# Blockwise attention and expert routing: ranks computed ahead of the scores, table compares on VectorE, zeros and the first v cast on ScalarE

## The chip, the cores and the metric

The kernel runs on one core of one Trainium2 chip. A core has five engines with queues of their own: TensorE (PE in the profile; its weight loads are PEld), VectorE (DVE), ScalarE (ACT), GpSimd (POOL) and SyncE (SP). SP, ACT and POOL also issue DMA transfers, all of which run on the same 16 DMA engines. The metric is device time in microseconds (us); several executions are timed and their median is taken. One execution is recorded by the hardware profiler, and every duration below is from that one.

## The reference

Attention has batch 8, 8 heads, 576 tokens and head dimension 64. A query sees a key if its block of 64 tokens is not before the key's block. The result becomes 4608 rows of 512, and each row goes through the two matrices of the expert that its domain number names:

```python
scores = np.where(block_i >= block_j, scale * q @ k.T, -1e9)
attn = softmax(scores)                       # float32
x = (attn @ v).transpose(0, 2, 1, 3).reshape(B * S, H * D)   # 4608 x 512
for e in range(8):                           # w1[e]: 512 x 1024, w2[e]: 1024 x 512
    mask = domain_id == e
    out[mask] = np.maximum(x[mask] @ w1[e], 0.0) @ w2[e]
```

All inputs and outputs are float32 (domain numbers are 64-bit integers); the kernel computes in float16 with float32 sums.

## The kernel before

The order of the work on each engine is the order in which the program writes it; no planner moves anything.

**Attention** is a loop over 32 pairs of heads (`p`, four pairs to a batch `b`) and a 33rd round that only finishes. A round of pair p contains, in this order: `emit_G(0)`, the first scores of p by TensorE and their exp by ScalarE; `emit_T(p + 2)`, the transposition of q and k of the pair after next by TensorE (L292) with two copies by VectorE (L296, tile QK); `emit_G(1)`; `emit_P`, the products with v of the pair before (L355, L360); `emit_G(2)`; `emit_Q`, the rest of them, then the reciprocal (L376) and the scaling (L377) into x by VectorE. After the last pair of a batch x is stored to the DRAM tensor x_rows by SP. In the last pair of a batch `emit_VE` (L386) copies part of the next batch's v into the tile VE by VectorE.

**Loads.** q and k are loaded by POOL with a cast to float16 (`load_qk`, four transfers a batch), v in float32 (`load_v`, five a batch) into vst, and cast to vS by `cast_v` (three instructions): for batch 0 by VectorE, for others by POOL. `loads(p)`, at the end of a round, writes batch b's loads at p = 4b - 10 and the cast of batch b - 1 between them. At p = 20 and 22 it issues the weights of experts 0 and 1, eight transfers each.

**Routing** (`routing`, a generator of which each round takes one step from p = 5) computes for each token its rank within its expert: a one-hot tile me, two matmuls (with ones_sq and the triangle up) that count over partitions, a scan on VectorE (L255), three POOL instructions (L259, L260, L264), a sum (L267), and `slot_col` (L211 to L224), integer arithmetic that makes the column u_f and the place lo_h of each token.

**The table** (`table`, `inverse`, one step a round from p = 19) inverts this: for each quarter of the tokens POOL builds one-hot tiles Hq (L165, L168), Hh (L170, L174) and L (L178, L182) by subtracting and comparing with zero, TensorE multiplies them (L188) and VectorE adds up (L193, L195). The result tok0 says which token stands in each of 128 x 40 slots, five blocks of 128 for each expert. L168, L170 and L182 are POOL's compares and its product.

**Experts.** POOL gathers the tokens of an expert from x_rows (L479, an indirect DMA for each block), TensorE transposes them (L489), VectorE copies (L492), `mm1` multiplies by w1 (L511) with relu by ScalarE (L517), `mm2` by w2 (L528); VectorE copies each block to a buffer osb (L534), POOL scatters it to the output (L535). Within mm2 POOL also issues the weights of expert e + 3 and TensorE transposes the next expert's tokens. For an expert with more than 640 tokens a loop from L590 makes further rounds; here it makes none.

Of the kernel before, what the change touches and what calls it, by code (L numbers as in the profile page):

```python
# [9 lines left out]
F32 = mybir.dt.float32  # L10
F16 = mybir.dt.float16
I32 = mybir.dt.int32
AF = mybir.ActivationFunctionType
ALU = mybir.AluOpType
# [4 lines left out]
def kernel(  # L19
# [54 lines left out]
    def load_v(eng, b, cs):  # L74
        for c in cs:
# [4 lines left out]

    load_qk(0, 0, 1)
    load_v(nc.sync, 0, range(5))
    nc.sync.dma_start(
        out=dom_i[:],
        in_=moe_domain_id.bitcast(I32).rearrange("(p c) -> p c", p=128))

    identh = const.tile([128, 128], F16, name="identh")
    make_identity(nc, identh[:])
    load_qk(0, 1, HP)
    up = const.tile([128, 128], F16, name="up")  # L90
    make_upper_triangular(nc, up[:], 1.0, diag=False)
    iota_h = const.tile([128, 128], F16, name="iota_h")
    nc.gpsimd.iota(out=iota_h[:], pattern=[[1, 128]], base=0, channel_multiplier=0,
                   allow_small_or_imprecise_dtypes=True)
    p_f = const.tile([128, 1], F32, name="p_f")
    nc.gpsimd.iota(out=p_f[:], pattern=[[0, 1]], base=4, channel_multiplier=NJ,
# [40 lines left out]
    cnt = const.tile([128, E], F32, name="cnt")  # L137
    tok0 = const.tile([128, 2, E * NB], I32, name="tok0")
    for i in range(3):
        nc.vector.memset(vS[i][:, :, :, 1:131:129], 1.0)  # L140
    for i in range(2):
        nc.vector.memset(ATE[i][:, 0:64], 1.0)
        nc.vector.memset(ATE[i][:, 64:832], 0.0)
        nc.vector.memset(VE[i][:], 0.0)
        nc.vector.memset(VE[i][0:64, :, :, 1:2], 1.0)
        nc.vector.memset(VE[i][64:128, :, :, 130:131], 1.0)
    po = aps.tile([128, 2, 512], F32, name="po")
    nc.vector.memset(po[:, 1, 264:396], 1.0)

    def inverse(sb, pp, tag, ncols, base, tok):
# [3 lines left out]
        inv = sb.tile([128, 2, ncols], F32, name="inv", tag="inv")  # L157
        yield
        for qt in range(4):
            js = slice(NQ * qt, NQ * qt + NQ)  # L160
            L = sb.tile([128, NQ, 128], F16, name="L", tag="L", bufs=2)
            Hq = sb.tile([128, NQ, ncols], F16, name="Hq", tag="Hq", bufs=2)
            Hh = sb.tile([128, NQ, 2, ncols], F16, name="Hh", tag="Hh", bufs=2)
            sh = [128, NQ, ncols]
            nc.gpsimd.tensor_tensor(  # L165
                out=Hq[:], in0=iota_h[:, 0:ncols].unsqueeze(1).to_broadcast(sh),
                in1=ub[:, js].unsqueeze(2).to_broadcast(sh), op=ALU.subtract)
            nc.gpsimd.tensor_scalar(  # L168
                out=Hq[:], in0=Hq[:], scalar1=0.0, scalar2=None, op0=ALU.is_equal)
            nc.gpsimd.tensor_scalar(  # L170
                out=Hh[:, :, 0], in0=Hq[:], scalar1=p_f[:, 0:1], scalar2=None,
                op0=ALU.mult)
            yield
            nc.gpsimd.tensor_tensor(  # L174
                out=Hh[:, :, 1], in0=Hq[:],
                in1=iota_h[:, js].unsqueeze(2).to_broadcast(sh), op=ALU.mult)
            sl = [128, NQ, 128]
            nc.gpsimd.tensor_tensor(  # L178
                out=L[:], in0=iota_h[:].unsqueeze(1).to_broadcast(sl),
                in1=lo_h[:, js].unsqueeze(2).to_broadcast(sl), op=ALU.subtract)  # L180
            yield
            nc.gpsimd.tensor_scalar(  # L182
                out=L[:], in0=L[:], scalar1=0.0, scalar2=None, op0=ALU.is_equal)
            yield
            ps = pp.tile([128, 512], F32, name=tag, tag=tag, bufs=2)
            pv = ps[:, 0 : 2 * ncols]
            for j in range(NQ):
                nc.tensor.matmul(  # L188
                    out=pv, lhsT=L[:, j], rhs=Hh[:, j].rearrange("p a c -> p (a c)"),
                    start=(j == 0), stop=(j == NQ - 1))  # L190
            fi = inv[:].rearrange("p a c -> p (a c)")
            if qt == 0:
                nc.vector.tensor_copy(out=fi, in_=pv)  # L193
            else:
                nc.vector.tensor_tensor(out=fi, in0=fi, in1=pv, op=ALU.add)  # L195
        nc.vector.tensor_tensor(
            out=inv[:, 0], in0=inv[:, 0], in1=inv[:, 1], op=ALU.add)
# [30 lines left out]
    def routing():  # L228
        nc.vector.memset(ones_sq[:], 1.0)
        dom_f = asb.tile([128, NJ], F16, name="dom_f")  # L230
# [3 lines left out]
            out=me[:], in0=iota_h[:, 0:E].unsqueeze(2).to_broadcast([128, E, NJ]),  # L234
            in1=dom_f[:].unsqueeze(1).to_broadcast([128, E, NJ]), op=ALU.is_equal)
        msk = asb.tile([128, E, NJ], F16, name="msk")
        nc.vector.memset(msk[:], 1.0)
        nc.vector.memset(msk[:, :, 0:1], 0.0)
        yield
        yield  # L240
        fl = "p e j -> p (e j)"
        nj = E * NJ
        ps_t = aps.tile([128, 512], F32, name="PT", tag="PT", bufs=2)
        ps_r = aps.tile([128, 512], F32, name="PT", tag="PT", bufs=2)
        nc.tensor.matmul(out=ps_t[:, 0:nj], lhsT=ones_sq[:],
                         rhs=me[:].rearrange(fl), start=True, stop=True)
        nc.tensor.matmul(out=ps_r[:, 0:nj], lhsT=up[:],
                         rhs=me[:].rearrange(fl), start=True, stop=True)
        rt = asb.tile([128, E, NJ], F32, name="rt")
        nc.scalar.copy(out=rt[:].rearrange(fl), in_=ps_t[:, 0:nj])  # L250
        rr = asb.tile([128, E, NJ], F32, name="rr")
        nc.scalar.copy(out=rr[:].rearrange(fl), in_=ps_r[:, 0:nj])
        yield
        inc = asb.tile([128, E, NJ], F32, name="inc")
        nc.vector.tensor_tensor_scan(  # L255
            out=inc[:].rearrange(fl), data0=msk[:].rearrange(fl),
            data1=rt[:].rearrange(fl), initial=0.0, op0=ALU.mult, op1=ALU.add)
        rk = asb.tile([128, E, NJ], F32, name="rk")
        nc.gpsimd.tensor_tensor(out=rk[:], in0=inc[:], in1=rt[:], op=ALU.subtract)  # L259
        nc.gpsimd.tensor_tensor(out=rk[:], in0=rk[:], in1=rr[:], op=ALU.add)  # L260
        yield
        nc.vector.tensor_scalar(out=cnt[:], in0=inc[:, :, NJ - 1], scalar1=-1.0,
                                scalar2=None, op0=ALU.add)
        nc.gpsimd.tensor_tensor(out=rk[:], in0=rk[:], in1=me[:], op=ALU.mult)  # L264
        yield
        rank = asb.tile([128, NJ], F32, name="rank")
        nc.vector.tensor_reduce(out=rank[:], in_=rk[:].rearrange("p e j -> p j e"),  # L267
                                axis=AX.X, op=ALU.add)
        yield
        ri = slot_col(asb, rank[:], dom_f[:], NJ, u_f[:], "t")  # L270
# [3 lines left out]
        nc.vector.tensor_copy(out=lo_h[:], in_=lo_i[:])  # L274
        yield
        nc.vector.memset(base_f[:], 0.0)
# [120 lines left out]

    npair = B * HP
    QKs = {0: emit_T(0)}
    rout, tabl = routing(), table()  # L400

    w1s, w2s = {}, {}


    def loads(p):
        fn = nc.gpsimd.tensor_copy
        for b in range(2, B):
            if p == max(0, 4 * b - 10):
                load_qk(b)
                load_v(nc.gpsimd, b, range(0, 3))  # L410
                cast_v(fn, b - 1)
                load_v(nc.gpsimd, b, range(3, 5))
        if p == 4 * B - 12:
            w1s[0], t1 = load_w1(wsb, 2, moe_w1[0])
            w2s[0], t2 = load_w2(wsb, 2, moe_w2[0])
            for f in t1:
                f()
            cast_v(fn, B - 1)
            for f in t2:
                f()  # L420
        if p == 4 * B - 10:
            w1s[1], t1 = load_w1(wsb, 2, moe_w1[1])
            w2s[1], t2 = load_w2(wsb, 2, moe_w2[1])
            for f in t1 + t2:
                f()

    prev = None
    for p in range(npair + 1):
        b, hp = divmod(p, HP)
        st = None  # L430
        if p < npair:
# [4 lines left out]
            emit_G(0, st)  # L436
        if p == 0:
            QKs[1] = emit_T(1)
            cast_v(nc.vector.tensor_copy, 0)
            emit_VE(0)  # L440
        elif p + 2 < npair:
            QKs[p + 2] = emit_T(p + 2)
# [6 lines left out]
        if prev is not None:  # L449
# [5 lines left out]
            elif prev["p"] % HP == HP - 1:  # L455
                store_x(prev, 0, DM, nc.sync)
        if p == 0:
            QKs[2] = emit_T(2)
        if p < npair and hp == 3 and b + 1 < B:
            emit_VE(b + 1)  # L460
        if p > 4:
            next(rout, None)
        if p > 18:
            next(tabl, None)
        loads(p)
        prev = st
    for _ in tabl:
        pass
    att.close()

# [51 lines left out]
    def mm2(hT, w2h, tok, dst, todo=(), nxt=None):  # L522
        if nxt is not None:
            transpose_block(*nxt, 0)
        for blk in range(NB):
# [5 lines left out]
            if nxt is not None and blk + 1 < NB:  # L531
                transpose_block(*nxt, blk + 1)
            osb = msb.tile([128, DM], F32, name="osb", tag="osb", bufs=6)
            nc.vector.tensor_copy(out=osb[:], in_=po[:])  # L534
# [102 lines left out]
```

## Time and profile before

| what | value |
|---|---|
| median of 14 runs | 346.28 us (341.71 to 348.49) |
| profiled execution, its own time | 343.2 us |
| its span | 341.4 us |
| granted TensorE clock, mean | 0.912 |
| busy: PE, DVE, ACT, POOL | 268.3, 157.0, 141.0, 227.2 us |
| last scaling of x (L377) ends | 158.2 us |
| first gather (L479) starts | 161.4 us |
| first matmul of expert 0 (L511) starts | 168.2 us |
| last scatter (L535) starts | 327.3 us |

A row of a timeline has the start, the duration (of a run of equal instructions from its first start to its last end), engine, line and operation, the tiles out<-in with partitions x elements, the count, and in brackets the idle time of the engine before it with what ended it. A row of a group has, after the count, its busy time and the mean nanoseconds of one, and after the second bar the idle time before. A row of the waits has the total, how often, and the longest. The granted clock is a share of full speed.

### The profile page before, as it was taken

Reading aid. Unit: us, or ns where it says so; the run is one execution under the profiler, and the core shown is the slowest. Engines: PE = TensorE matmul, PEld = TensorE weight load, DVE = VectorE, ACT = ScalarE, POOL = GpSimd, SP = SyncE. Lnnn points to the kernel's source line nnn. Section 1 sums busy time; section 2 is a strip of 40 time slices with the busy share of each in tenths; the row PEclk is TensorE's granted clock in tenths of the full one; section 3 lists DMA queues with packets and bytes.
Section 4 is the critical chain, followed back from the end, with each engine's and each line's share of the span. In section 5 each row is a group of like instructions: output and inputs, shape, how many; then the busy total and the mean of one; then the engine's idle time right before and its main releaser. Section 6 shows DMA issues by size and latency. Waiting matters only on the chain. (4 is left out here: it accounts for less than half of the span.)

```text
span 341.4 us, 8495 instructions
## 1 busy us (share of the span) xinstructions
PE 268.3 (79%) x3622; PEld 176.2 (52%) x3622; DVE 157.0 (46%) x277; ACT 141.0 (41%) x203; POOL 227.2 (67%) x273
## 2 busy tenths in 40 slices
PE   1589688768699297582589998989799899999920
PEld 1357456546466275462355665647465464756500
DVE  5467788878568956943102523040230504042210
ACT  1358758828678266470042331505123060514200
POOL 8758557986629999970787858787777775232220
PEclk9999989969989679785599999999999999999975
DMA  9999999999965996022369996989899695112120
GB/s 174 199 212 222 211 224 202 198 220 252 210 198 106 206 184 144 2 72 69 94 127 220 223 231 144 238 193 222 228 186 223 143 225 182 58 61 76 63 80 0
DMA packets 36023, 55.66 MB, mean 163 GB/s; under 512 B 9390, under 2 KB 22190, under 8 KB 35984
## 3 DMA queue, kind: packets, MB, share of 16 engines
q0 software_dynamic: 25680, 49.17, 68.9%
q1 hardware_dynamic: 9776, 5.81, 6.4%
q8 instruction: 29, 0.48, 0.6%
q10 hardware_dynamic: 528, 0.13, 0.2%
q14 instruction: 10, 0.08, 0.1%
HBM read 67.15 MB, written 15.20 MB: 241 GB/s over the span
## 5 line engine op out<-in xcount | busy, mean ns | idle before, releaser
L309 ACT ACTIVATE A<-ps 128x1024 f16<-128x1024 f32 (+1 forms) x96 | 82.9, 884 | 58.8 <-PE ps L304 46.5
L517 ACT ACTIVATE hT<-ph 128x640 f16<-128x640 f32 (+1 forms) x72 | 46.3, 644 | 117.8 <-PE ph L511 95.4
L528 PE MATMUL po<-w2h,hT 128*128 128x512 f16 x320 | 74.9, 379 | 6.0 <-DVE osb L534 4.9
L511 PE MATMUL ph<-xT,w1h 128*128 128x320 f16 x512 | 73.7, 304 | 1.8 <-issue 1.1
L535 POOL DMA_INDIRECT out_dram<-osb,tok x40 | 40.7, 1018 | 46.3 <-DVE osb L534 31.4
L492 DVE COPY xT<-pt 128x512 f16<-128x512 f16 x40 | 16.9, 424 | 105.5 <-PE pt L489 75.2
L511 PEld LDWEIGHTS <-w1h 128*128 128x128 f16 x512 | 50.8, 99 | 24.5 <-issue 2.2
L479 POOL DMA_INDIRECT xg<-x_rows,tok x40 | 40.5, 1013 | 22.5 <-issue 10.9
L296 DVE COPY QK<-PT 128x576 f16<-128x576 f16 x64 | 45.6, 750 | 9.3 <-PE PT L292 9.0
L528 PEld LDWEIGHTS <-hT 128*128 128x128 f16 x320 | 30.1, 98 | 36.1 <-issue 6.7
L360 PE MATMUL po<-vS,A 128*128 128x65 f16 x640 | 38.5, 205 | 5.4 <-issue 5.4
L77 POOL DMA_DIRECT2D vst<-in_v_dram x35 | 30.6, 879 | 14.3 <-DMA vst<-in_v_dram 7.5
L304 PE MATMUL ps<-QK 64*128 64x512 f16 (+3 forms) x256 | 37.0, 331 | 1.5 <-DVE QK L296 0.9
L360 PEld LDWEIGHTS <-A 128*128 128x128 f16 x640 | 33.6, 105 | 7.2 <-issue 7.1
L534 DVE COPY osb<-po 128x512 f32<-128x512 f32 x40 | 27.3, 683 | 18.9 <-PE po L528 18.2
L355 PE MATMUL po<-VE,ATE 128*128 128x130 f16 x160 | 34.0, 238 | 2.3 <-DVE x L377 2.2
L292 PE MATMUL PT<-identh,qh 64*64 64x64 f16 x576 | 17.7, 207 | 18.7 <-DVE QK L296 10.4
L377 DVE TENSOR_TENSOR x<-po,rc 128x768 f16<-128x768 f32 x32 | 30.6, 957 | 1.1
L292 PEld LDWEIGHTS <-qh 64*64 64x64 f16 x576 | 14.1, 120 | 27.0 <-issue 18.5
L489 PE MATMUL pt<-identh,xg 128*128 128x128 f16 x160 | 15.9, 226 | 8.4 <-issue 7.6
L292 PE MATMUL PT<-identh,kh 64*64 64x64 f16 x576 | 17.2, 204 | 5.4 <-issue 2.9
L355 PEld LDWEIGHTS <-ATE 128*128 128x128 f16 x160 | 16.3, 102 | 9.6 <-issue 7.3
(83 smaller groups left out, 244.5 us busy)
## 6 DMA issues: line engine op xcount, KB each, us to landing
w1h<-in_moe_w_dram POOLq DMA_DIRECT2D x32, 256.0 KB
w2h<-in_moe_w_dram POOLq DMA_DIRECT2D x32, 256.0 KB
vst<-in_v_dram POOLq DMA_DIRECT2D x28, 256.0 KB
qh<-in_q_dram POOLq DMA_DIRECT2D x14, 288.0 KB
kh<-in_k_dram POOLq DMA_DIRECT2D x14, 288.0 KB
x_rows<-x SPq DMA_DIRECT2D x7, 512.0 KB, 10.7
vst<-in_v_dram SPq DMA_DIRECT2D x4, 256.0 KB, 4.9
vst<-in_v_dram POOLq DMA_DIRECT2D x7, 128.0 KB
```

Source lines behind the costliest of these rows:

```text
L77: eng.dma_start(out=vst[b % 3][0:n, c], in_=v[b, :, 128 * c : 128 * c + n, :].rearrange("h p d -> p h d"))
L292: nc.tensor.transpose(out=PT[h, j], in_=src[h, hp, 64 * j : 64 * j + 64], identity=identh[h, h])
L296: nc.vector.tensor_copy(out=QK[:, s].rearrange("p (n j) -> p n j", j=9), in_=PT[:].rearrange("p j n -> p n j"))
L304: nc.tensor.matmul(out=o[:, i], lhsT=QK[h, 1, 128 * c : 128 * c + 128], rhs=QK[h, 0, 64 + 128 * c : S], start=True, stop=True)
L309: nc.scalar.activation(out=o, in_=i, func=AF.Exp, scale=0.125)
L355: nc.tensor.matmul(out=o[:, 1:131], lhsT=st["AE"][:, 128 * m : 128 * m + 128], rhs=VE[b % 2][:, m, hp, 1:131], start=True, stop=(m == 0))
L360: nc.tensor.matmul(out=o[:, 1 + 65 * i : 66 + 65 * i], lhsT=at_block(st, i, c, m), rhs=vS[b % 3][:, c, hp, 1 + 65 * i : 66 + 65 * i], star ...
L479: nc.gpsimd.indirect_dma_start(out=g[:, blk, :], out_offset=None, in_=xd, in_offset=bass.IndirectOffsetOnAxis(ap=tok[:, 1, blk : blk + 1], ...
L511: nc.tensor.matmul(out=ph[:, i, 0:hw], lhsT=w1_cols(w1h, dc, fc), rhs=xT[:, dc, hw * i : hw * i + hw], start=(dc == 0), stop=(dc == 3))
L517: nc.scalar.activation(out=hT[:, fc].rearrange("p (i n) -> p i n", i=2)[:, i0:i1], in_=ph[:, i0:i1, 0:hw], func=AF.Relu)
L528: nc.tensor.matmul(out=po[:], lhsT=hT[:, fc, 128 * blk : 128 * blk + 128], rhs=w2h[:, fc, :], start=(fc == 0), stop=(fc == 7))
L535: nc.gpsimd.indirect_dma_start(out=dst[blk], out_offset=bass.IndirectOffsetOnAxis(ap=tok[:, 0, blk : blk + 1], axis=0), in_=osb[:], in_off ...
```

## The change

- **Start.** The domain numbers are now SP's first transfer, ahead of v. POOL makes iota_h first, then identh and up, and only then loads q and k of pairs 1 to 3. The zeros in VE and ATE are written by ScalarE as copies of one zero, seen as float32; the ones in VE come later, in `emit_ones`.
- **Routing** has two steps, taken before the loop: the first (one-hot tile and the two count matmuls, into a `ps` tile) ahead of `emit_T(0)`, the second after it. It reads the counts from PSUM directly, and all its arithmetic is on VectorE, without the two ScalarE copies and the three POOL instructions.
- **First pair.** The transposition of pair 1 and VE of batch 0 come after all scores of pair 0, and the cast of batch 0's v is made by ScalarE.
- **Table.** A quarter is split into `differ` (two subtractions on POOL), `equal` (two compares and a product on VectorE), `column` (a product on POOL) and `add` (the matmuls, and a sum on VectorE), which follow each other in successive rounds; a new quarter begins every second round, from p = 18.
- **Weights** of experts 0 and 1 are issued two transfers a round from p = 20.
- **Between attention and experts** 36 matmuls of 128x512 are added whose results nobody reads.
- **osb** has ten buffers in place of six.

```diff
-    load_qk(0, 0, 1)
-    load_v(nc.sync, 0, range(5))
     nc.sync.dma_start(
         out=dom_i[:],
...
+    load_qk(0, 0, 1)
+    load_v(nc.sync, 0, range(5))
...
+    z_f = const.tile([128, 1], F32, name="z_f")
+    nc.vector.memset(z_f[:], 0.0)
+    nc.vector.memset(ones_sq[:], 1.0)
+    for i in range(2):
+        n = 5 * HP * 66
+        nc.scalar.copy(
+            out=VE[i][:].rearrange("p m g z -> p (m g z)").bitcast(F32),
+            in_=z_f[:].to_broadcast([128, n]))
+        nc.scalar.copy(out=ATE[i][:, 64:832].bitcast(F32),
+                       in_=z_f[:].to_broadcast([128, 384]))
...
-        nc.vector.memset(ATE[i][:, 64:832], 0.0)
-        nc.vector.memset(VE[i][:], 0.0)
...
+        def differ(qt):
...
             nc.gpsimd.tensor_tensor(
                 out=Hq[:], in0=iota_h[:, 0:ncols].unsqueeze(1).to_broadcast(sh),
                 in1=ub[:, js].unsqueeze(2).to_broadcast(sh), op=ALU.subtract)
+            nc.gpsimd.tensor_tensor(
+                out=L[:], in0=iota_h[:].unsqueeze(1).to_broadcast(sl),
+                in1=lo_h[:, js].unsqueeze(2).to_broadcast(sl), op=ALU.subtract)
+
+        def equal(qt):
+            L, Hq, Hh = ts[qt]
+            nc.vector.tensor_scalar(
                 out=Hq[:], in0=Hq[:], scalar1=0.0, scalar2=None, op0=ALU.is_equal)
+            nc.vector.tensor_scalar(
+                out=L[:], in0=L[:], scalar1=0.0, scalar2=None, op0=ALU.is_equal)
+            nc.vector.tensor_scalar(
                 out=Hh[:, :, 0], in0=Hq[:], scalar1=p_f[:, 0:1], scalar2=None,
                 op0=ALU.mult)
+
+        def column(qt):
...
             nc.gpsimd.tensor_tensor(
                 out=Hh[:, :, 1], in0=Hq[:],
                 in1=iota_h[:, js].unsqueeze(2).to_broadcast(sh), op=ALU.mult)
...
+        for k in range(10):
+            for d, f in ((3, add), (2, column), (1, equal), (0, differ)):
+                if (k - d) % 2 == 0 and 0 <= k - d < 8:
+                    f((k - d) // 2)
+            yield
...
+    rout, tabl = routing(), table()
+    next(rout)
     QKs = {0: emit_T(0)}
+    emit_ones()
+    next(rout)
...
+            cast_v(fn, B - 1)
+            for e in range(2):
+                w1s[e], w2s[e], t = load_weights(wsb, 2, moe_w1[e], moe_w2[e])
+                wts.extend(t)
+        for f in wts[:2]:
+            f()
+        del wts[:2]
...
         if p == 0:
+            cast_v(nc.scalar.copy, 0)
+            QKs[1] = emit_T(1)
+            emit_VE(0)
             QKs[2] = emit_T(2)
...
-        if p > 4:
-            next(rout, None)
-        if p > 18:
+        if p > 17:
             next(tabl, None)
...
+    ps = aps.tile([128, 2, 512], F32, name="ps", tag="ps", bufs=2)
+    for i in range(36):
+        nc.tensor.matmul(out=ps[:, i % 2], lhsT=identh[:], rhs=w1s[0][:, 0, 0:512],
+                         start=True, stop=True)
...
-            osb = msb.tile([128, DM], F32, name="osb", tag="osb", bufs=6)
+            osb = msb.tile([128, DM], F32, name="osb", tag="osb", bufs=10)
```

## The prediction

> **What bounds the kernel now.** The chain that ended last holds only the final scatter, so the stages were read instead: first busy time by stretch (columns: window, length, then busy us and count of PE, PEld, DVE, ACT, POOL; granted clock, DMA share, GB/s).
>
> ```profile
> 100.00:113.00 13.00, 12.13 (x324) 8.94 (x322) 11.48 (x21) 11.78 (x18) 10.36 (x15) 1.00 0.55 108
> 113.00:121.00 8.00, 2.13 (x44) 1.59 (x46) 6.53 (x5) 0.87 (x2) 7.90 (x8) 0.57 1.02 187
> 132.00:144.00 12.00, 7.75 (x204) 5.84 (x206) 9.56 (x11) 6.65 (x9) 11.64 (x9) 0.89 0.14 44
> 165.00:168.00 3.00, 1.80 (x12) 1.15 (x13) 1.15 (x3) 0.00 (x0) 2.23 (x3) 0.50 0.37 107
> 171.00:174.00 3.00, 3.00 (x19) 1.85 (x17) 0.00 (x0) 1.31 (x3) 2.39 (x3) 0.81 0.39 107
> ```
>
> In the undisturbed stretch PE, DVE and ACT are all nearly full and a pair of heads takes 3.0 us (the x results of L377 end 3.0 apart). In 113 to 121 and 132 to 144 POOL alone is full and PE is not: that is the table. From 165 the experts begin at clock 0.50. Next, the order of time around the gaps, and the two waits that matter later:
>
> ```profile
> 113.72 5.43 DVE L386 COPY VE<-vS 64x1280 f16<-64x1280 f16 x2
> 113.29 2.16 POOL L178 TENSOR_TENSOR L<-iota_h,lo_h 128x1152 f16<-128x1152 f16 x1
> 115.55 3.26 POOL L182 TENSOR_SCALAR L<-L 128x1152 f16<-128x1152 f16 x1
> 118.87 0.78 PE L188 MATMUL PT<-Hh,L 128*128 128x80 f16 x9 [6.33 <-POOL L L182]
> 71.48 0.69 PE L292 MATMUL PT<-identh,qh 64*64 64x64 f16 x18 [4.21 <-DVE QK L296]
> 102.44 0.78 POOL L165 TENSOR_TENSOR Hq<-iota_h,ub 128x360 f16<-128x360 f16 x1 [6.40 <-DVE ub L155]
> 161.44 1.16 POOL L479 DMA_INDIRECT xg<-x_rows,tok  x1 [10.11 <-DMA x_rows<-x]
> 168.18 6.04 PE L511 MATMUL ph<-xT,w1h 128*128 128x320 f16 x28 [0.52 <-issue]
> PE po L528 <- DVE osb L534: 4.9, 3, 1.8
> ```
>
> The two VE copies, 0.49 us each elsewhere, stood behind one POOL instruction each; PE stood behind the table (6.33) and behind routing on DVE (4.21). The gather waits for the last store, not for the table. The costs per form:
>
> ```profile
> L182 POOL TENSOR_SCALAR L<-L 128x1152 f16<-128x1152 f16 x4 | 12.8, 3189 | 0.4
> L178 POOL TENSOR_TENSOR L<-iota_h,lo_h 128x1152 f16<-128x1152 f16 x4 | 8.5, 2122 | 0.0
> L170 POOL TENSOR_SCALAR Hh<-Hq,p_f 128x360 f16<-128x360 f16 x4 | 4.8, 1190 | 0.4
> L168 POOL TENSOR_SCALAR Hq<-Hq 128x360 f16<-128x360 f16 x4 | 4.5, 1115 | 0.4
> L165 POOL TENSOR_TENSOR Hq<-iota_h,ub 128x360 f16<-128x360 f16 x4 | 3.4, 862 | 6.4 <-DVE ub L155 6.4
> L174 POOL TENSOR_TENSOR Hh<-Hq,iota_h 128x360 f16<-128x360 f16 x4 | 3.2, 804 | 0.0
> ```
>
> **1. Start: gain 1 us (-2 to +3).** dom_i goes ahead of v on SP: one issue of 0.79 us, so v lands 0.8 later; its last piece was issued at 3.86 and took 10.3 (the longest landing), so about 16 now. The iota, moved up, and the upper triangle, 0.24 + 0.5 us, now precede the q and k of pairs 1 to 3 on POOL. First transposes waited for q until 5.5 and 6.3; the two count matmuls now stand before them and need dom_i. In before dom_i took 9.0 us to land, behind five v loads; alone, nearer v's shortest 3.3: 4.5 to 5, then cast and compare of 0.7 (0.2 + 0.5; the rows' 2.08 and 0.79 ran under POOL's v cast). So no delay to 1 us; at 9.0 it would be 5. The zeros leave DVE (3.1 us) for ScalarE: two of 1320 and two of 384 elements, by exp's 597 ns at 512 and 1027 at 1024, 2 x (1.28 + 0.49) = 3.5 us, over at 5.7 after the table load, under the wait for q; the first exp came at 10.25. Ranks and slots, about 4.5 us of DVE (scan 0.75, reduce 0.64, three products 0.5 each, nine small at 0.2), end near 14, when QK of pair 1 was waiting for q and k anyway. The v cast on ScalarE takes 2 x 1.03 + 0.6 = 2.7 us after exp of pair 0 and ends near 17 (DVE's ended 17.4). The rest of pair 0's scores no longer queues behind pair 1's transposes, so the first x ends near 24 instead of 25.
>
> **2. Routing out of the loop: gain 8 us (6 to 9.5).** Against 3.0 per pair: pair 5 took 5.9, of which 1.15 is PE's own issue gap (stays), 1.7 goes; pairs 6 and 7 ran with a cooled clock and a VE copy, 1.2 goes; pair 10, waiting for rank, 0.8; pair 11 took 8.0 with 3.4 us of slot arithmetic on DVE (67.3 to 70.7), the rest being a VE copy that stays; pair 12, cold after it, 1.0. Sum 8.1. The five x stores are not moved.
>
> **3. The table: gain 4 us (-8 to +16).** From the end of x of pair 17 (97.3) to that of pair 31 (158.2) before takes 60.8 us for 14 pairs; at 3.05 they are 42.7. Off POOL come 3.19 + 1.19 + 1.12 = 5.5 us a quarter, four times 22 us. On DVE come three 16-bit compares or products. The nearest row is the VE copy, 1280 elements in 0.49: L's 1152 cost 0.45, the two of 360 0.25 each, 0.95 a quarter (1.3 if the strided product runs at a quarter of that rate). DVE already has QK 1.41 + 0.23 + 0.96 = 2.6 of a pair's 3.0, VE another 1.0 every fourth, so about 5 us become path.
>
> Here a rule speaks against the change. The row: a VE copy took 2.09 and 3.33 us under L178 and L182. The Trainium skill, SBUF — State Buffer, "SBUF: two separate sides", says that VectorE's two-port modes and GpSimd lock one port pair exclusively for a whole instruction. The row shows that DVE gets in between two POOL instructions. By the row's mean wait of (2.09 + 3.33)/2 - 0.49 = 2.2, twelve compares would add 27 us; by the rule only while POOL computes, so no more than its remaining 4 x 3.8 + two casts of 2.6 = 20 us, and less, since the compares wait for the subtraction anyway. I take some 3 us of it within the following.
>
> What is late next is POOL. Its first subtraction needs ub, which DVE makes at p = 18, and now stands ahead of batch 7's loads; before, those were issued from 81.4 on and the 6.40 idle came after them. With T the end of x of pair 17: subtractions to 3.3, q and k (4 x 0.62) to 5.8, three v loads to 8.5, cast of v 6 (2.6) to 11.1, two v to 12.7, column 0 to 13.5, subtractions 1 to 16.5, cast of v 7 to 19.1 (its v landed by 16 to 18), four of the weight loads at 0.57 to 21.3, column 1 and subtractions 2 to 25.1, two weights a pair from there. PE wants column 0 at T+10 and has it at 13.5; DVE's compare 1 waits to 16.5, under the cast to 19; x of pair 21 ends near T+21.7 where 14 was due, x of 23 near 30 behind compare 2, after that POOL keeps up. With DVE's own additions x of pair 31 ends at T+56, PE once more cooled T+57: 60.8 - 57 = 4. The other end is no POOL stall at all, T+45.
>
> The weight loads of experts 0 and 1 (16 issues, 0.57 each) are spread two a pair to p = 27; needed at the experts' start, 30 us later: nothing. The table is then finished at p = 28, ahead of the store; the gather still follows the last store by 3.3 us.
>
> **4. The 36 matmuls: gain 2.4 us (-5 to +3).** They run from 1.2 us before the last x (E) until the gather's first tokens are transposed at E+7.0. The first half of expert 0, 32 matmuls, took 7.3 us (168.18 to 175.5), the second 4.95. By the row the clock rose some 5 us after dense work began at 168: 12 at 0.43 and 24 at 0.216 = 10.3 us, to E+9.1, when the third block's data arrives anyway (E+8.9). The Trainium skill, TensorE: Matmul & The Clock Gate, "What's actually happening", gives 3.4 us: 8 cold, 9.5 us, E+8.3. Either hides the overrun; if the clock stayed at 0.50, 15.4 us would cost 5.
>
> **5. Ten osb: gain 4.5 us (0 to 6.9).** Experts 1 to 5 take 19.5, 20.1, 20.4, 20.2, 19.0 us from one first transposition to the next, expert 0's rows 18.5 (mm1 8.7, then 5 x 1.95): excess 6.9. Each time DVE is late, an osb copy follows that reuses a buffer scattered 19 to 29 us earlier. Ten buffers put 40 us there. Against all of it: the DMA queues at 0.88 to 0.97 and POOL at 17.6 of 20 us an expert leave little room for a faster pace.
>
> **Sum.** 1 + 8 + 4 + 2.4 + 4.5 = 19.9. The profiled execution took 343.2 (span 341.4), so 323.3; it lies 3.1 below the median of the runs, 346.28, where the forecast is 326.4.
>
> **Rivals.**
> (a) POOL is never late: casts and loads of batch 7 slip through while PE is behind. For it: POOL idles before T, with the queue empty. Against it: its work of 12.7 us in the time of four pairs. 8 to 12 more: 314 to 318.
> (b) The table's wait only moves: v 7 lands 15 us later, since scatters sat about 20 us in a full queue, and cast 7 holds column 1. 326.4 + 12 = 338. Against it: the queue drains before T.
> (c) Slower, by the same mechanism: cast 7 in POOL's order ahead of column 1 and subtractions 2 stops PE and DVE. It costs one us for each us that v lands after T+18; at 20 later (T+38, 25 us after its issue at 12.7) the whole gain is gone, at 25 the time is 351. Landings in the expert stage come up to this, in the attention stage none is shown.
> (d) No change: the gain of steps 2 and 3 is given back because DMA, at 1.07 to 1.15 until 100 us, sets the pace. Against it: PE never waits for q or k after the start. 345 to 348.
>
> **How the numbers follow.** Forecast 0.58 (own range 318 to 335), (a) 0.15, (b) 0.14, (d) 0.03, (c) 0.10. About 0.5%, 1.7 us, can be told from no change. Faster: 0.58 + 0.15 + 0.14 = 0.87; same 0.03; slower 0.10. The range reaches over (b) and most of (a), 315 to 342.
>
> **What would show it.** DVE's slot arithmetic before 15 us and no PE gap like 4.21 near 70; x of pair 17 near 88; a POOL wait for ub ahead of batch 7's loads, and a PE or DVE gap of 3 to 8 us two to five pairs after it; x of pair 31 near 145; clock 1.00 at the first mm1; 18.5 to 19 us per expert. It is wrong if pairs 19 to 24 lose over 20 us, if dom_i lands after 8 us, or if experts keep 20 us.

## The result and the profile after

The changed kernel takes **335.96 us** (median of 10 runs, 333.23 to 339.25) where the kernel before takes 345.28 (47 runs). The ratio is 0.9764, with an interval of 0.973 to 0.9798: 2.4% or 8 us are gained (9.3 between the medians), where the prediction's steps added up to 19.9. The time lies within the range of 315 to 342, which reaches over rival (b) and most of (a), and just outside the 318 to 335 of the forecast itself; the gain is less than half of what was forecast.

The profiled execution of the changed kernel took 340.5 us (span 338.7), 4.5 above the median, so a second profile of the same kernel (run `e1_after`, 332.8 us, span 330.9) is read beside it. Single executions of one kernel lie up to 10 us apart (337.28 to 347.28 in e2_osb10), which is more than most of the effects in question; where that matters, means over several profiles are given.

The busy time by stretch of the changed kernel (columns as in the prediction):

```profile
100.00:113.00 13.00, 9.72 (x209) 7.14 (x210) 10.99 (x18) 5.98 (x9) 11.48 (x13) 0.74 0.93 209
128.00:141.00 13.00, 11.16 (x282) 8.25 (x277) 10.18 (x21) 9.38 (x13) 3.07 (x5) 0.87 0.99 200
158.00:161.00 3.00, 1.74 (x11) 0.63 (x9) 0.00 (x0) 0.00 (x0) 2.12 (x3) 1.00 0.30 90
161.00:168.00 7.00, 4.52 (x32) 2.84 (x33) 1.27 (x3) 1.99 (x5) 5.44 (x6) 1.00 0.32 94
```

In the table's first half POOL is still the full engine (11.48 of 13) and TensorE still is not (9.72, clock 0.74). The later half now runs: POOL has only 3.07 of 13 us to do, TensorE 11.16. At 161 the experts begin at a granted clock of 1.00 (the third number from the end) in this execution, and yet TensorE is busy for only 4.52 of 7 us.

The timeline of the changed kernel around the table (POOL, VectorE and TensorE, in order of time):

```profile
93.72 0.79 POOL L179 TENSOR_TENSOR Hq<-iota_h,ub 128x360 f16<-128x360 f16 x1 [10.32 <-DVE ub L166]
96.52 1.27 POOL L69 DMA_DIRECT2D qh<-in_q_dram  x2
98.40 1.81 DVE L190 TENSOR_SCALAR L<-L 128x1152 f16<-128x1152 f16 x1
101.63 2.64 POOL L105 CAST vS<-vst 128x1024 f16<-128x1024 f32 x3
105.73 0.86 POOL L199 TENSOR_TENSOR Hh<-Hq,iota_h 128x360 f16<-128x360 f16 x1
106.64 0.76 PE L208 MATMUL PT<-Hh,L 128*128 128x80 f16 x9 [1.32 <-POOL Hh L199]
107.23 2.16 POOL L182 TENSOR_TENSOR L<-iota_h,lo_h 128x1152 f16<-128x1152 f16 x1
107.59 2.89 DVE L188 TENSOR_SCALAR Hq<-Hq 128x360 f16<-128x360 f16 x1
109.28 1.08 POOL L105 CAST vS<-vst 128x1024 f16<-128x1024 f32 x1
116.54 3.58 DVE L400 COPY VE<-vS 64x1280 f16<-64x1280 f16 x2
120.31 0.24 DVE L188 TENSOR_SCALAR Hq<-Hq 128x360 f16<-128x360 f16 x1
120.44 0.58 PE L306 MATMUL PT<-identh,kh 64*64 64x64 f16 x18 [2.72 <-DVE inv L214]
```

POOL stood still for 10.32 us before its first subtraction and only then issued batch 7's loads (from 96.52); from there it worked without a pause until column 0 (L199), which came 12.2 us after x of pair 17 (93.5). TensorE waited for it, and 2.72 us for the sum of the second quarter (L214), which stood on VectorE behind the VE copies of 3.58 us. VectorE's compares took 2.89 and 1.81 us where POOL was at work, and 0.24 and 0.45 elsewhere. At the 1.81 us POOL computed nothing: it issued the loads of k and v. At 120.31 it issued weights, and the compare took 0.24.

### The profile page after: what moved, and what is told of

Read it like the earlier page. It is cut to its first block, busy times and chain, and to the rows that moved or that the text cites. A ratio compares the mean times of both kernels' runs of the same rounds, so it can differ in the third digit from the quotient of the medians.

```text
span 338.7 us, 8559 instructions
## 1 busy us (share of the span) xinstructions
PE 273.9 (81%) x3658; PEld 176.9 (52%) x3658; DVE 153.0 (45%) x286; ACT 146.8 (43%) x208; POOL 203.3 (60%) x258
## 5 line engine op out<-in xcount | busy, mean ns | idle before, releaser
L542 PE MATMUL po<-w2h,hT 128*128 128x512 f16 x320 | 76.6, 385 | 6.5 <-DVE osb L548 4.4
L525 PE MATMUL ph<-xT,w1h 128*128 128x320 f16 x512 | 72.1, 299 | 3.7 <-DVE xT L506 1.9
L525 PEld LDWEIGHTS <-w1h 128*128 128x128 f16 x512 | 50.0, 98 | 25.5 <-issue 3.8
L374 PE MATMUL po<-vS,A 128*128 128x65 f16 x640 | 36.9, 201 | 4.4 <-issue 4.4
L374 PEld LDWEIGHTS <-A 128*128 128x128 f16 x640 | 32.2, 103 | 6.7 <-issue 6.7
L369 PE MATMUL po<-VE,ATE 128*128 128x130 f16 x160 | 33.0, 233 | 2.8 <-DVE x L391 2.8
L390 DVE RECIPROCAL rc<-po 128x12 f32<-128x12 f32 x32 | 7.4, 231 | 31.8 <-PE po L369 31.8
```

Of the source, the lines that this page charges most:

```text
L369: nc.tensor.matmul(out=o[:, 1:131], lhsT=st["AE"][:, 128 * m : 128 * m + 128], rhs=VE[b % 2][:, m, hp, 1:131], start=True, stop=(m == 0))
L374: nc.tensor.matmul(out=o[:, 1 + 65 * i : 66 + 65 * i], lhsT=at_block(st, i, c, m), rhs=vS[b % 3][:, c, hp, 1 + 65 * i : 66 + 65 * i], star ...
L525: nc.tensor.matmul(out=ph[:, i, 0:hw], lhsT=w1_cols(w1h, dc, fc), rhs=xT[:, dc, hw * i : hw * i + hw], start=(dc == 0), stop=(dc == 3))
L542: nc.tensor.matmul(out=po[:], lhsT=hT[:, fc, 128 * blk : 128 * blk + 128], rhs=w2h[:, fc, :], start=(fc == 0), stop=(fc == 7))
```

## The experiments

The end of x of a pair is that of its scaling; x17 and x31 stand for pairs 17 and 31, and the stage of the experts for the time from x31 to the start of the last scatter. Times are medians; the kernel before was run beside each group: 343.0 (first group, e1 to e4, 13 runs), 342.31 (second, e5 to e8, 6), 335.54 (third, e9 to e12, 7), 344.19 (fourth, e13 to e16, 7). The ratio is the one to go by; it can differ a little from that of the medians.

| run | us | ratio to before | x17 | x31 | experts |
|---|---|---|---|---|---|
| before, first profile | 346.28 | 1 | 97.3 | 158.2 | 169.2 |
| after, first profile | 335.96 | 0.9764 (0.973 to 0.9798) | 93.5 | 152.9 | 172.1 |
| e1_after | 333.85 | 0.9769 (0.9707 to 0.9831) | 92.1 | 151.0 | 165.8 |
| e2_osb10 | 341.85 | 0.992 (0.9852 to 0.9988) | 92.6 | 156.1 | 166.8 |
| e3_no36 | 333.51 | 0.9759 (0.9676 to 0.9841) | 92.0 | 151.7 | 166.1 |
| e4_early | 338.52 | 0.9888 (0.9796 to 0.998) | 92.2 | 151.8 | 167.0 |
| e5_table | 334.67 | 0.9824 (0.9653 to 0.9995) | 94.2 | 153.3 | 165.6 |
| e6_before_noload | 332.55 | one run | 89.3 | 148.7 | 167.8 |
| e7_after_noload | 325.5 | one run | 84.4 | 142.7 | 166.9 |
| e8_noweights | 333.22 | one run | 91.0 | 150.0 | 171.8 |
| e9_loads_first | 321.53 | 0.9624 (0.9531 to 0.9718) | 95.2 | 145.4 | 160.3 |
| e10_first_fill | 321.63 | 0.962 (0.953 to 0.971) | 96.7 | 145.3 | 160.5 |
| e11_nogather | 317.61 | one run | 89.7 | 143.9 | 160.5 |
| e12_osb6 | 325.11 | 0.9729 (0.9635 to 0.9823) | 94.3 | 145.1 | 161.8 |
| e13_before | 344.3 | one run | 97.3 | 157.0 | 171.4 |
| e14_after | 338.35 | 0.9842 (0.9796 to 0.9888) | 90.6 | 150.6 | 174.0 |
| e15_loads_first | 332.57 | 0.964 (0.9579 to 0.9701) | 98.5 | 150.4 | 167.6 |
| e16_after_osb6 | 339.0 | 0.985 (0.9793 to 0.9908) | 94.5 | 153.3 | 171.0 |

**Which part brings what.** The first question was how the 8 us divide. e1_after is the changed kernel again, beside four kernels that hold a part of the change. e2_osb10 is the kernel before with ten buffers:

```diff
-            osb = msb.tile([128, DM], F32, name="osb", tag="osb", bufs=6)
+            osb = msb.tile([128, DM], F32, name="osb", tag="osb", bufs=10)
```

e3_no36 is the changed kernel without the 36 matmuls:

```diff
-    ps = aps.tile([128, 2, 512], F32, name="ps", tag="ps", bufs=2)
-    for i in range(36):
-        nc.tensor.matmul(out=ps[:, i % 2], lhsT=identh[:], rhs=w1s[0][:, 0, 0:512],
-                         start=True, stop=True)
```

e4_early keeps only the new start and the routing ahead of the loop; the table, its place in the loop, the weight loads, the six buffers and the end of attention are those of before (one line of the edit is shown):

```diff
-        if p > 17:
+        if p > 18:
             next(tabl, None)
```

e5_table is the kernel before with only the new table and, as the table needs POOL, the weight loads two a round (one line of it again):

```diff
-        if p > 18:
+        if p > 17:
             next(tabl, None)
```

> The changed kernel as it is, profiled again beside the three below. 9 to 10 us faster than the kernel before (ratio 0.973 to 0.980). If TensorE's own gaps in the attention stage ('issue' in the timeline) set where the routing gain went, they sum to over 10 us before the x of pair 17 here too, against 9 in the kernel before.

> The kernel before with ten osb buffers and nothing else. The prediction's step 5: 4.5 us faster (0 to 6.9). Rival, read from the changed profile, where the late copies stand at the same places with ten buffers: the late copies are not waits for a buffer, and the time is that of before within 1.5 us.

> The changed kernel without the 36 matmuls. The prediction's step 4: 2.4 us slower than the changed kernel, so 338.4 where that has 336. Rival: the clock gained is given back in gaps before the second half of expert 0, and the two differ by less than 1 us.

> Start, early routing and the new order of pair 0 only: table, weight issues, osb of before and no 36 matmuls. The prediction's steps 1 and 2: 9 us faster than before. Rival: most of it comes back as TensorE's own gaps while DMA is full until the loads of batch 7 are done, so 3 to 4 us faster, as the x of pair 17 is in the changed profile (93.5 against 97.3).

> The kernel before with the new table (split between POOL and VectorE, from pair 18) and the spread weight issues, nothing else. The prediction's step 3: 4 us faster. Rival (b), that the waits only move to POOL's later subtractions and to locked VectorE copies, as the changed profile has them (1.8, 2.9 and 3.6 us on three VectorE instructions that take 0.45, 0.24 and 1.0 alone): within 1.5 us of before.

The start and the early routing (e4_early) are worth 1.1% or 3.8 us, with an interval of 0.7 to 6.9; 9 were forecast. From there to the whole change (e1_after) it is another 1.2%, 4.1 us, though the two intervals overlap. Of these the 36 matmuls bring nothing that shows (333.51 without them, 333.85 with them, each known to some 3 us). The ten buffers gave 2.7 us on the kernel before (e2_osb10, 0.4 to 5.1); further down they give nothing in the changed kernel. What is left of the 4.1 us is the table, forecast at 4. The table alone on the kernel before (e5_table) gave 6 us, but between 0.2 and 12. So, as far as these intervals allow, the deficit of 12 us sits in steps 2, 4 and 5, and not in the table, which had the widest bounds.

**Where step 2's gain went.** In the profile of before TensorE's stall of 4.21 us behind routing was plain, and it is gone: the last integer operation of routing now ends at 15.5 us. But x17 did not come 9 us earlier. The early kernels whose batch 7 is loaded at the old place (e4, e9, e10, e11, e12, e15) have x17 at 94.4 in the mean of six, the kernels with routing in the loop (before, e2, e13) at 95.7 in the mean of three. The changed kernel and its variants with the same order (after, e1, e3, e8, e14, e16) have 92.3; they load batch 7 later.

What stands in the place of the stalls are issue gaps, in which TensorE waited for no semaphore that the profile shows. From the timeline of TensorE of the changed kernel (the bracket is the gap before the row):

```profile
47.59 0.40 PE L318 MATMUL ps<-QK 64*128 64x384 f16 x4 [2.28 <-issue]
67.27 0.22 PE L306 MATMUL PT<-identh,qh 64*64 64x64 f16 x3 [2.02 <-issue]
74.02 0.28 PE L344 MATMUL ps<-QK 64*64 64x64 f16 x7 [1.85 <-issue]
80.76 0.31 PE L306 MATMUL PT<-identh,kh 64*64 64x64 f16 x8 [2.12 <-issue]
```

In this part they come about every 6.7 us, and always at the same places of TensorE's instruction stream. The busy time from the start to each of these four gaps counts the matmuls first and the weight loads second:

```profile
0.00:47.58 47.58, 32.55 (x735) 22.98 (x736) 32.83 (x73) 31.36 (x41) 32.93 (x53) 1.00 1.08 210
0.00:67.26 67.26, 48.69 (x1119) 34.55 (x1120) 45.65 (x93) 45.77 (x61) 46.49 (x71) 0.97 1.08 211
0.00:74.01 74.01, 53.58 (x1247) 38.14 (x1248) 49.59 (x99) 49.61 (x66) 52.69 (x79) 0.98 1.08 217
0.00:80.75 80.75, 58.20 (x1375) 41.55 (x1376) 55.03 (x106) 54.33 (x73) 57.35 (x84) 0.98 1.09 216
```

From gap to gap it is 3, 1 and 1 times 128 matmuls, or 256 instructions with their weight loads. Between 24 and 100 us the 18 profiles hold 120 issue gaps of over 0.15 us; every one stands at such a place, and none elsewhere. The profile also shows what arrives there. Its list of DMA queues (packets, MB, share of the 16 engines) has for the changed kernel

```profile
q8 instruction: 30, 0.49, 0.6%
```

These are 30 packets of 16 KB. TensorE's 3658 matmuls and as many weight loads make 28.6 blocks of 256 instructions, and each of the 120 gaps ends 1.2 to 1.9 us after one of them has landed. What TensorE waits for is its own next block of instructions, which comes through the same DMA engines as the loads. The packet ahead of a gap begins 3.9 us (median; 2.5 to 5.9) after the place before.

The sum of the gaps between 24 and 100 us is 9.5, 5.7, 10.5 and 5.1 in the four profiles with routing in the loop (mean 7.7) and 7.7 to 16.4 in the twelve with early routing (mean 11.6). So in the mean 4 us that routing's stalls gave back came out again as issue gaps, though single profiles lie far apart. A stall gives the next block time to arrive: in before the two places behind the stall of 4.21 us, at 71.9 and 78.5 us, have no gap. Where the stall is taken out, TensorE reaches these places sooner. To see what makes the packets late, the loads of q, k and v of batches 4 to 7 were left out of both kernels (e6_before_noload, e7_after_noload; those batches then compute with old data), so that the DMA queues run dry at some 50 us:

```diff
-                load_qk(b)
-                load_v(nc.gpsimd, b, range(0, 3))
+                if b < 4:
+                    load_qk(b)
+                    load_v(nc.gpsimd, b, range(0, 3))
...
-                load_v(nc.gpsimd, b, range(3, 5))
+                if b < 4:
+                    load_v(nc.gpsimd, b, range(3, 5))
```

> The kernel before without the loads of q, k and v for batches 4 to 7 (their attention uses older batches, so it is not the reference's). If full DMA queues make TensorE's own gaps in the attention stage, these shrink from over 9 us before pair 17's x to under 5, and routing on VectorE then costs its full 8 us. If not, the gaps stay.

> The changed kernel without the same loads. If the gaps swallowed the routing gain, its x of pair 17 now comes 6 to 9 us ahead of that of the kernel before without the loads. If they did not, the distance stays at 1 to 4 us, as with the loads.

The gaps fell to 3.2 and 4.0 us, all of them before 50 us, while loads were still in the queues. From 52 us on the packet begins 0.7 us (median) after the place before, and there is no gap. x17 now stands 4.9 us apart (89.3 and 84.4) instead of 1 to 3. That is less than the 6 to 9 expected: in these two executions some 4 of the 9 us of steps 1 and 2 were not to be had even where the gaps were gone. Busy time from 60 to 90 us (columns as above) in the changed kernel as it is:

```profile
60.00:90.00 30.00, 21.76 (x566) 15.92 (x566) 20.84 (x31) 19.41 (x28) 17.77 (x22) 1.00 0.99 208
```

and in the changed kernel without those loads (e7_after_noload):

```profile
60.00:90.00 30.00, 28.82 (x763) 21.38 (x761) 26.60 (x44) 27.45 (x40) 7.89 (x8) 1.00 0.13 43
```

Same kernel, same clock of 1.00; with the DMA share at 0.99 TensorE did 566 matmuls, at 0.13 it did 763. Leaving out the loads also makes POOL's work less (17.77 to 7.89 us), and with it what VectorE waits for, so not all of the 763 is due to the gaps. Nor does a high share alone make them: from 128 to 141 us, with weights in the queues, it is 0.99 as well (the second row of the result), and no issue gap of over 0.15 us stands there.

**The table's waits.** If POOL's order is what makes the table late, the cure is to put batch 7's loads back ahead of the first subtraction, and not behind it. e9_loads_first and e15_loads_first are the changed kernel with that alone, run in the third and fourth group:

```diff
+        if p == 18:
+            loads(p)
         if p > 17:
             next(tabl, None)
-        loads(p)
+        if p != 18:
+            loads(p)
```

e14_after and e13_before are the two kernels unchanged, for profiles of the same group as e15.

> The changed kernel with one move: at p = 18 batch 7's loads and the cast of v 6 are written ahead of the first subtractions. If step 3's chain is right (POOL, entered late, holds column 0 and compare 1 at pair 21 and column 1 and compare 2 at pair 23), the pairs 21 and 23, 9.7 and 8.3 us in the changed kernel's second profile, fall to under 5 together with the wait of TensorE for Hh, and 6 to 9 us are gained on the changed kernel: ratio to before about 0.955. Rival: the waits are the port's, and move to other places; no more than 2 us gained.

> Batch 7's loads ahead of the first subtractions, again. If the table's waits are what it takes away (the stretch from pair 17 to 31 was 50.2 us against 58.9), it is 5 to 8 us faster than the changed kernel on the same chip, and faster than both kernels. If its lower ratio was the chip's, within 2 us.

> The changed kernel, for the comparison with the next on one chip: ratio to before 0.977.

> The kernel before, profiled beside the three below on the same chip. If the late copies among the experts belong to the chip or the moment and not to six buffers, its experts take 18.4 us each where the others' do; if to six buffers, it has 19 to 20 where those with ten have 18.4.

The same chip in the same group gives 0.964 for e15 and 0.9842 for e14 (0.977 was expected): 5.8 us between the medians, with intervals that lie apart. It beats both kernels. The table's timeline with the loads first (e9_loads_first):

```profile
95.39 0.79 POOL L179 TENSOR_TENSOR Hq<-iota_h,ub 128x360 f16<-128x360 f16 x1 [2.58 <-DVE ub L166]
106.12 0.25 DVE L188 TENSOR_SCALAR Hq<-Hq 128x360 f16<-128x360 f16 x1
```

In the fourth group, the busy time from 90 to 120 us in the changed kernel (e14_after):

```profile
90.00:120.00 30.00, 20.51 (x466) 14.91 (x458) 24.34 (x39) 16.39 (x22) 27.91 (x33) 0.80 0.75 148
```

its TensorE at the table's first quarter, in the timeline:

```profile
103.75 0.76 PE L208 MATMUL PT<-Hh,L 128*128 128x80 f16 x9 [3.91 <-POOL Hh L199]
```

and the same stretch with the loads first (e15_loads_first):

```profile
90.00:120.00 30.00, 25.75 (x645) 18.92 (x644) 24.61 (x48) 22.36 (x32) 25.12 (x29) 0.95 0.72 154
```

POOL's wait for ub shrinks from 10.32 (first profile) to 2.58 (e9), the compare that took 2.89 us takes 0.25, the PE wait of 3.91 us in e14 is gone in e15, and from 90 to 120 TensorE does 645 matmuls instead of 466 at a clock of 0.95 instead of 0.80. Pairs 21 and 23, in which TensorE stood behind the table, took 9.1 and 9.4 us in e14 and take 3.9 and 5.4 in e15. The 14 pairs after pair 17 take 51.2 us in the mean of five such kernels (e9 to e12, e15) and 59.3 in six with the changed order. Against that, batch 7's loads then come before pair 17, and x17 is 2.6 later (94.9 against 92.3), which leaves 5.5 at x31, close to the 5.8 that were timed. One reservation: most of those five profiles are from the third group, in which the kernel before was faster too; e15's own x31 is level with e14's (150.4 and 150.6). In that pair of profiles the 14 pairs are 8.1 us shorter, x17 is 7.9 later, and the difference in time stands in the stage of the experts. The 5.8 us are measured, and that the table's waits went is seen in both; that they are what the 5.8 us consist of is supported by the means, not by every pair.

**The first matmuls of expert 0.** The 36 matmuls ran as forecast, and still brought nothing. TensorE's timeline in the changed kernel (e1_after):

```profile
149.60 7.93 PE L481 MATMUL ps<-w1h,identh 128*128 128x512 f16 x36
158.82 0.38 PE L503 MATMUL pt<-identh,xg 128*128 128x128 f16 x4 [1.28 <-issue]
...
160.83 0.61 PE L503 MATMUL pt<-identh,xg 128*128 128x128 f16 x4 [0.99 <-DMA xg<-x_rows,tok]
161.95 7.23 PE L525 MATMUL ph<-xT,w1h 128*128 128x320 f16 x32 [0.52 <-DVE xT L506]
```

its busy time by stretch:

```profile
158.00:160.00 2.00, 0.78 (x8) 0.47 (x8) 0.54 (x2) 0.00 (x0) 1.70 (x2) 1.00 0.36 104
160.00:166.00 6.00, 4.66 (x20) 2.70 (x21) 0.73 (x2) 1.31 (x3) 4.48 (x6) 0.50 0.33 98
166.00:169.00 3.00, 2.96 (x18) 1.76 (x17) 0.00 (x0) 1.31 (x3) 2.69 (x4) 0.86 0.36 97
```

and the same 32 matmuls in the timeline of e9_loads_first:

```profile
155.91 5.06 PE L528 MATMUL ph<-xT,w1h 128*128 128x320 f16 x32 [0.52 <-DVE xT L509]
```

The clock had not cooled at the end of attention, so the 36 took 7.9 us (36 x 0.22) and not the forecast 10.3, and ended 1.3 us before the first transposition. Then TensorE had 12 small transpositions with gaps of 1.28, 0.24 and 0.99 us, and at 160 the clock fell to 0.50: the first 32 matmuls took 7.23 us, as in before (7.3). In e9 with nearly the same gaps the clock stayed at 1.00 and they took 5.06. In the first profile of the changed kernel the clock stayed up too, but two issue gaps of 0.92 and 0.75 us fell among the 32, which took 6.9. So a held clock is worth up to 2.2 us by the rows, and not in every execution; in time e3_no36 shows none of it. e10_first_fill closes the gaps, on the kernel with the loads first:

```diff
-    for i in range(36):
+    for i in range(42):
...
+            warm = mps.tile([128, 512], F32, name="po", tag="po", bufs=2)
...
+                    for _ in range((1, 4, 2, 0, 0)[blk]):
+                        nc.tensor.matmul(out=warm[:], lhsT=identh[:],
+                                         rhs=w1s[0][:, 0, 0:512], start=True, stop=True)
```

> The same, and 42 idle matmuls instead of 36, with four and two more behind the transposition of expert 0's second and third block. If step 4 failed because the clock fell back in the gaps between the last of the 36 and the first mm1 (0.50 again from 160 to 166), the clock now stays at 1.00, the first half of expert 0 takes 4.9 to 5.3 instead of 7.2, and 2 us are gained on the run before this one. Rival: the idle matmuls delay the transpositions by as much.

It held the clock (5.06 us) and changed nothing in the time: 321.63 against 321.53, since in e9's profile the clock held without it as well. It did not hold in all of that group: in e12_osb6 the 32 matmuls took 6.46 us, at a granted clock of 0.83 from 153 to 163.

**The ten buffers and the late copies.** The prediction read 6.9 us of lateness in the copies to osb, and took the buffers for the cause. e12_osb6 is e9_loads_first, and e16_after_osb6 the changed kernel, with six buffers:

```diff
-            osb = msb.tile([128, DM], F32, name="osb", tag="osb", bufs=10)
+            osb = msb.tile([128, DM], F32, name="osb", tag="osb", bufs=6)
```

> As the first of these, with six osb buffers instead of ten. By the prediction's step 5 it is 4.5 us slower than with ten; by the changed profile, where late copies stand at the same places with ten, within 1.5 us; by the run of before with ten buffers, 2.7 slower.

> The changed kernel with six osb buffers. Step 5 as predicted: 4.5 us slower than the changed kernel. If the late copies are not waits for a buffer: within 1.5 us.

e16 and e14, same chip and group, are 0.985 and 0.9842: no difference (medians 0.65 us apart). From the waits (total us, times, longest us) of the changed kernel with ten buffers (e14_after):

```profile
PE po L542 <- DVE osb L548: 6.7, 4, 2.2
```

and with six (e16_after_osb6):

```profile
PE po L542 <- DVE osb L548: 3.8, 3, 2.1
```

TensorE waits for late copies with ten buffers as with six, about 2 us at a time. Where the longest of e14's waits begins can be followed in its timeline:

```profile
198.44 0.39 PE L503 MATMUL pt<-identh,xg 128*128 128x128 f16 x4
201.96 0.43 DVE L506 COPY xT<-pt 128x512 f16<-128x512 f16 x1 [3.29 <-PE pt L503]
202.31 0.68 DVE L548 COPY osb<-po 128x512 f32<-128x512 f32 x1
203.04 2.95 PE L542 MATMUL po<-w2h,hT 128*128 128x512 f16 x8 [2.20 <-DVE osb L548]
```

In VectorE's order the copy to osb stood behind a copy to xT, and that one waited 3.29 us for a transposition whose row ends at 198.83. The lateness was there before a buffer was asked for. e12 and e9 (0.9729 and 0.9624) have overlapping intervals, though their medians are 3.6 us apart. In their profiles every expert but the last takes 18.4 us, with six buffers as with ten, so the buffers do not explain the 3.6 there. In the profiles of the other groups the seven steps from one expert's first copy to the next's add up to 134.6 us with six buffers (mean of six) and 134.3 with ten (mean of eight). That leaves nothing for the buffers, and the 2.7 us of e2_osb10 without a cause. In those groups, e13_before among them, it is 18.4 in one expert and 19 to 23 in the next: between the first osb copies of successive experts, the first profile of the changed kernel has 18.4, 19.4, 20.5, 23.3, 20.2, 17.8 and 17.7. Two runs looked for the cause in the transfers of this stage. In e8_noweights experts 3 to 7 compute with the weights of expert 2, in e11_nogather (on e9) they compute with the tokens gathered for experts 0 and 1:

```diff
-            w1s[e + 3], w2s[e + 3], todo = load_weights(
-                msb, 4, moe_w1[e + 3], moe_w2[e + 3])
+            w1s[e + 3], w2s[e + 3] = w1s[2], w2s[2]
```

```diff
-            xgs[e + 2] = gather(tok_of(e + 2))
+            xgs[e + 2] = gather(tok_of(e + 2)) if e == 0 else xgs[e % 2]
```

> The changed kernel without the weights of experts 3 to 7 (they use those of expert 2, so the output is not the reference's). If the late copies among the experts come from full DMA queues, every expert from 2 on takes 18.4 us from first transposition to the next. If they come from waiting for POOL or for a buffer, some stay at 19 to 21.

> As the first of these, but experts 3 to 7 use the tokens gathered for experts 0 to 2 (not the reference's output); weights are all loaded. If the late copies among the experts come with the gathers, experts 1 to 5 now take 18.4 us each. If they come with the scatters or the weights or TensorE's own stream, some stay at 19 to 20.

Without the weight loads the experts still took 23.2, 19.1, 19.9, 19.6, 19.2, 18.4 and 17.7 us, so the weight loads are not the cause either. Without the gathers they took 18.4 each, but so did e9 beside it, and the run tells nothing apart. What makes a transposition's end come 2 to 3 us late to VectorE in most experts of one execution, and in none of another, stays open.

## Why the prediction was wrong

The sign was right, and the time's place in a wide range; the sum was not: 8 us against 19.9.

1. **Start: right.** 1 us was forecast; x of pair 0 ends at 24.5 in the first profile and 23.8 in the second, against 25.0. dom_i had landed by 2.78 us, before the bound of 4.5; the zeros took 3.6 us on ScalarE (two of 1.29, two of 0.51; 3.5 was worked out), and its v cast 2.50 (2.7).
2. **Routing: the size failed.** The step added up the stalls of pairs 5 to 12, 8.1 us in all, and kept the issue gaps at "stays". The stalls went and the gaps grew by 4 us in the mean. Steps 1 and 2 together were timed at 3.8 us (0.7 to 6.9). The sentence that failed is the one that set each pair against the 3.0 us of an undisturbed one: that pace was read at a DMA share of 0.55, while pairs 5 to 12 run at about 1.1, where TensorE's own instructions come late. And not all that those pairs lost was routing's, since the two kernels were only 4.9 us apart at x17 without the loads. Rival (d) said that DMA sets the pace until 100 us and dismissed it because TensorE never waits for q or k. It was half right, and the argument against it looked at the wrong sign: the cost showed as issue gaps, not as a wait for data.
3. **Table: the mechanism was right, step by step.** POOL was entered late (10.32 us for ub, ahead of batch 7's loads); column 0 came at T+12.2 (T+13.5 forecast); x21 at T+20.1 and +20.2 (21.7), x23 at T+32.0 and +31.5 (30), x31 at T+59.4 and +58.9 (57). From T on the change saves 1.5 to 2 us against the 60.8 of before, where 4 were forecast; of the 6 us timed in e5_table (0.2 to 12) the rest is not placed by a profile. That the whole came near rival (b)'s 338 is chance. Rivals (a), (b) and (c) fell with the timeline: POOL was late, and v of batch 7 made POOL wait only 1.52 us. For the port the two views gave 27 and up to 20 us, and 3 were taken. In the first profile the compares took 0.93 and 0.79 us in the mean where 0.25 and 0.45 is the time alone (e9_loads_first), four each: 4.1 us. The exclusive port of the Trainium skill (SBUF — State Buffer, "SBUF: two separate sides") fits the 2.89 us compare beside POOL's subtraction of 2.16 and cast of 1.08, but a compare waits for one or two POOL instructions, not for POOL's whole run, and the one of 1.81 us stood beside issues of loads, which the bound "only while POOL computes" left out. What the prediction lacked here was the next thought: the late entry is a matter of order, and moving one call takes it away, for 5.8 us in e15.
4. **The 36 matmuls: failed, nothing that shows for 2.4.** The premise that they begin at a cooled clock was wrong (they ran at 0.22 us each from the first), and their end, 1.3 us before the data, left time for the clock to fall. The Trainium skill (TensorE: Matmul & The Clock Gate, "What's actually happening") counts windows of about 3.4 us that run freely: from 157.5 to 161.0 TensorE had little to do, and the clock was at 0.50 from 160 on in e1_after, and at 1.00 with almost the same gaps in e9_loads_first. That agrees with a window that falls differently from one execution to the next, but no run here shows where it fell.
5. **Ten osb: failed.** 4.5 us were forecast; in the changed kernel the buffers gave 0.65 us, within the noise, and on the kernel before 2.7 (0.4 to 5.1) that no profile places. The late copies were read as waits for a free buffer, because each reuses one scattered 19 to 29 us earlier. With ten they were as late. The bound of 0 should have been the value, since the waits of before list none of VectorE's copies to osb behind a scatter.

Shortfall by step: 5.2 of steps 1 and 2 (9 less 3.8), 2.4, and some 4 of step 5, together about 12, against 19.9 less 8. Each of these is known to some 3 us, so that the sum closes this well is partly luck.

## What to carry to other kernels

A stall that is taken out of a stretch with issue gaps is worth less than its length, because TensorE then reaches its next block of instructions sooner, and that block queues with the loads; take the pace for such a stretch from a row with the same loads in flight. To see whether issue gaps are of this kind, count the instructions between them. Where an engine's queue holds both a wait for a late value and loads that depend on nothing, write the loads first: on one chip the same change was worth 1.6% with them behind, and 3.6% with them ahead. A copy that is late beside a buffer's reuse is no proof of a shortage of buffers, unless the wait itself names the release.

## What was not expected of the hardware

TensorE's issue gaps of up to 3.9 us, 5 to 16 us in the 76 us from 24 to 100, stood multiples of 256 instructions apart without exception, and each ended within 2 us of the landing of a 16 KB packet of the instruction queue. Without the loads of q, k and v they were 3 to 4 us, all before 50 us. The granted clock, after 7.9 us of dense matmuls and gaps of 1.28 and 0.99 us between short transpositions, fell to 0.50 in one execution and stayed at 1.00 in another with gaps of 1.21 and 0.93: 7.23 against 5.06 us for the same 32 matmuls. And the stage of the experts, of nearly the same instructions, took from 160 to 174 us, in steps of about 2 us per expert.
